# Two casts moved to ScalarE, and the last batch's q and k transposed by DMA instead of TensorE

## The chip, the cores and the metric

The kernel runs on one core of one Trainium2 chip. A core has five engines that run their own instruction streams in order and meet through semaphores: TensorE (PE; its weight loads are listed apart as PEld), VectorE (DVE), ScalarE (ACT), GpSimd (POOL) and SyncE (SP). SP only issues DMAs here. POOL issues DMAs too, between its copies. The metric is the device time of one execution in microseconds (us).

## The reference

Two things are computed one after the other. First, attention with a causal window of 64 keys, for 8 batches, 8 heads, 576 positions and a head size of 64:

```
scores = scale * q @ k.T;  mask = (rel >= 0) & (rel < 64)      # rel = query - key
attn = softmax(where(mask, scores, -1e9));  x = attn @ v        # x as [4608 tokens, 512]
```

Then two dense layers over the 4608 tokens:

```
h = x @ w_in          # 512 -> 2048
g = h - tanh(h)
out = g @ w_out       # 2048 -> 512, float32
```

Inputs and output are float32; the kernel works in bfloat16 with float32 sums.

## The kernel before

**Units.** Heads are taken in pairs: `g = 4*b + pr` is pair `pr` of batch `b`, 32 pairs in all, and g = 28 to 31 are the last batch's. The tokens of a batch are 9 windows of 64. The dense layers work on chunks `c` of 512 tokens (9 chunks); a chunk's first layer is 16 blocks `m` of 4 matmuls (`hp_mm`, L366), then a tanh on ACT (L371) and a subtraction on DVE (`g_sub`, L378) that writes `gT`; its second layer is 16 steps of 4 matmuls (`yp_mm`, L390), and after every fourth a copy on ACT and a store issued by SP (`y_out`, L395 and L397).

**Order.** Nothing is planned by a scheduler: the order on each engine is the order in which the program emits. A loop at the end (L593) walks over half-steps `h` from 0 to 351. Each half-step emits one block of a dense layer (`OPS`: from h = 96 on an even h has a first-layer block, an odd one a second-layer step), then the attention work filed under that h with `at(h, ...)`, and, after a first-layer block, its `g_sub`. So a number given to `at` is a place in every engine's stream, not a time: an engine goes past it as soon as its waits allow. From chunk 2 on, first-layer blocks share two PSUM banks (`m % 2`), in chunk 1 three.

**Attention of one pair.** In the later batches (a is the pair's first half-step, L555 to L567):

- POOL casts q at `a - 7` and k at `a - 5` (`cast`, recorded as L84) from the loaded layout `[head, row, 6*64]` to rows `[96, 6, 128]`, into a tile of a pool of three (`qb`, `kb`).
- `tr` at `a` and `a + 2` (L228 to L239): 6 TensorE transposes (L232) into one PSUM bank. For q, ACT moves head 0's half and DVE head 1's half into `qT` (64x576 each, recorded as L82 and L84); `qT` has a second copy of the width, with zeros in each head's other half. For k, ACT moves 128x576 into `kT`.
- `scores` at a + 5, 7, 9 (3 matmuls L299 and an Exp L301 each), `masking` on DVE at a + 11 (L305), `pv` at a + 13, 14, 15 (3 matmuls L315 each), `norm` on DVE at a + 15 (a reciprocal L322 and two multiplications L326).

`kT` and `qT` each have two buffers, used by `g % 2`. Pairs start 8 half-steps apart: a = 188, 196, 204, 212 for the last batch. Once a batch's four pairs are done, its x is transposed for the first layer, from batch 4 on by two SP DMA transposes (`x_dma`, L347), for batch 6 at h = 196.

The early pairs use `tr_rows` (L247) and `tile_scores` (L262), with the unpadded `qs`: for pair 9, whose k and q were cast on POOL at h = 23 (`cast_pair(9, G)`, L535, ahead of the loads of `w_out` and of batch 3), `tr_rows` stands at 37 and 38 and `tile_scores` at 41 and 43. At h = 39 DVE copies half of batch 2's V windows (`shift_dve(2, 0, 4)`, two copies L154, 64x2080 bf16 from SBUF to SBUF).

**Loads.** POOL issues them. q and k of batch 7 are loaded whole (`load_all`, L98; 576 KB of bf16 each) at h = 168 and 171, its V at h = 158. Before each of these loads a `pace` (L427, recorded as L430) makes POOL wait until DVE has written the newest `gT` block.

**V.** POOL casts V into `vb` pair by pair (`cast_v`; batch 7 at h = 164, 169, 174, 179), nine SP DMAs `keys_v` (L148; batch 7 at h = 182 to 186) copy `vb` into the key windows `vw`, and one DMA `shift_v` (L156; h = 189) fills the other half. `VALUES` (L554) holds these places.

Of the kernel before, what the change touches and what calls it, by code (L numbers as in the profile page):

```python
# [8 lines left out]
BF16 = mybir.dt.bfloat16  # L9
# [6 lines left out]
def kernel(  # L16
# [9 lines left out]
    nc = tc.nc  # L26
    B, H, S, D = q.shape
    NP = H // 2
    NJ = S // 64
    E, P = 6, S // 6  # L30
# [12 lines left out]
    const = ctx.enter_context(tc.tile_pool(name="const", bufs=1))  # L43
# [4 lines left out]
    sm_pool = ctx.enter_context(tc.tile_pool(name="sm", bufs=3))  # L48
    xt_pool = ctx.enter_context(tc.tile_pool(name="xt", bufs=3))
    g_pool = ctx.enter_context(tc.tile_pool(name="g", bufs=2))  # L50
    psum = ctx.enter_context(tc.tile_pool(name="psum", bufs=1, space=PSUM))

    ps = psum.tile([128, 8, 512], F32, name="ps")
# [7 lines left out]
    WIDE = 1024, 1024  # L63
    w_in_sb = [const.tile([128, 4, n], BF16, name=f"wi{i}") for i, n in enumerate(WIDE)]
    w_out_sb = const.tile([128, M, d_model], BF16, name="w_out_sb")
    NR, NPT = 2, 4

    vw = [const.tile([128, NJ, H, D + 1], BF16, name=f"vw{i}") for i in range(2)]  # L70
    vb = const.tile([PV, EV, H, D + 1], BF16, name="vb")
    PT = [const.tile([128, NJ, 128], BF16, name=f"pt{i}") for i in range(NPT)]
    kT = [const.tile([128, 64 + S], BF16, name=f"kt{i}") for i in range(NR)]
    qT = [const.tile([128, 2, S], BF16, name=f"qt{i}") for i in range(NR)]
    qs = [const.tile([128, S], BF16, name=f"qs{i}") for i in range(2)]
    xs = [const.tile([128, NJ + 1, NP, D], BF16, name=f"xs{i}") for i in range(2)]

    stage, rows, whole = {}, {}, {}

    def move(eng, o, i):  # L80
        if eng is nc.scalar:
            nc.scalar.activation(o, i, ACT.Copy)  # L82
        else:
            eng.tensor_copy(o, i)  # L84
# [116 lines left out]
    for i in range(2):  # L201
        nc.vector.memset(kT[i][:, 0:64], 0.0)
    nc.vector.memset(vw[0][0:64, 0], 0.0)

# [13 lines left out]
    def tr_heads(g, which, bank, eng):  # L218

        src = stage.pop((g, which))  # L220
        tp = ps[:, bank, :].bitcast(BF16)[:, 0:E * P].rearrange("c (e p) -> c e p", e=E)
        for e in range(E):
            for h in range(2):
                nc.tensor.transpose(tp[64 * h:64 * h + 64, e, :], src[:, h, D * e:D * e + D], ident[:P, :P])
        o = qs[g % 2] if which == "q" else kT[g % NR][:, 64:]
        move(eng, o.rearrange("c (p e) -> c p e", e=E), tp.rearrange("c e p -> c p e"))

    def tr(g, which, bank, *engs):  # L228
        src = rows.pop((g, which)).rearrange("p e h d -> p e (h d)")
        tp = ps[:, bank, :].bitcast(BF16)[:, 0:E * P].rearrange("c (e p) -> c e p", e=E)  # L230
        for e in range(E):
            nc.tensor.transpose(tp[:, e, :], src[:, e, :], ident[:P, :P])  # L232
        t = tp.rearrange("c e p -> c p e")
        if which == "q":
            o = qT[g % NR].rearrange("c h (p e) -> c h p e", e=E)
            move(engs[0], o[0:64, 0], t[0:64])
            move(engs[1], o[64:128, 1], t[64:128])
        else:
            move(engs[0], kT[g % NR][:, 64:].rearrange("c (p e) -> c p e", e=E), t)  # L239

    def pair_of(banks):
        a, b = banks
        return ps[:, a:b + 1:b - a]
# [3 lines left out]
    def tr_rows(g, which, bank, eng):  # L247

        src = rows.pop((g, which)).rearrange("p e h d -> p e (h d)")
        tp = ps[:, bank, :].bitcast(BF16)[:, 0:E * P].rearrange("c (e p) -> c e p", e=E)  # L250
        for e in range(E):
            nc.tensor.transpose(tp[:, e, :], src[:, e, :], ident[:P, :P])
        o = qs[g % 2] if which == "q" else kT[g % NR][:, 64:]
        move(eng, o.rearrange("c (p e) -> c p e", e=E), tp.rearrange("c e p -> c p e"))

    def hides(grp, banks):
        n = GROUPS[grp][1]
        for h in range(2):
            nc.tensor.matmul(ps[:, banks[h], 0:64 * n], ident, hide[:, h].unsqueeze(1).to_broadcast([128, n, 64]),
                             start=True, stop=False)  # L260

    def tile_scores(g, grp, banks, how="hide"):  # L262

        j0, n = GROUPS[grp]
        if how == "hide":
            hides(grp, banks)
        for i in range(n):
            j = j0 + i
            for h in range(2):
                r = slice(64 * h, 64 * h + 64)  # L270
                nc.tensor.matmul(ps[:, banks[h], 64 * i:64 * i + 64], kT[g % NR][r, 64 * j:64 * j + 128],  # L271
                                 qs[g % 2][r, 64 * j:64 * j + 64], start=how == "mask", stop=how == "mask" or i == n - 1)
        o = PT[g % NPT][:, j0:j0 + n].rearrange("p j (h t) -> p h j t", h=2)
        nc.scalar.activation(o, pair_of(banks)[:, :, 0:64 * n].rearrange("p h (j t) -> p h j t", t=64),  # L274
                             ACT.Exp, scale=scale)
# [19 lines left out]
    def scores(g, grp, bank):  # L295
        sp = ps[:, bank, 0:384].rearrange("p (i q) -> p i q", i=3)
        for i in range(3):
            j = 3 * grp + i
            nc.tensor.matmul(sp[:, i, :], kT[g % NR][:, 64 * j:64 * j + 128],  # L299
                             qT[g % NR][:, :, 64 * j:64 * j + 64], start=True, stop=True)  # L300
        nc.scalar.activation(PT[g % NPT][:, 3 * grp:3 * grp + 3, :], sp, ACT.Exp, scale=scale)  # L301

# [121 lines left out]
    def at(h, fn, *args):  # L424
        items.setdefault(h, []).append((fn, args))
# [10 lines left out]
    V, A, G, Y = nc.vector, nc.scalar, nc.gpsimd, nc.sync  # L436
# [111 lines left out]
    at(76, x_tr, 2, 1, 0, 4, 3, V)  # L548
    at(78, x_tr, 2, 1, 4, 9, 3, A)

    LOADS = {4: (75, 77, 79), 5: (106, 109, 102), 6: (140, 144, 126), 7: (168, 171, 158)}
    STEPS = {2: (0, 0, 49, 57), 3: (72, 79, 86, 93), 4: (100, 107, 114, 121), 5: (128, 135, 142, 149)}
    TURNS = {13: (97, 3, 99, 3), 15: (110, 4, 111, 3)}
    VALUES = {3: (66, 1, 71), 4: (88, 1, 93), 5: (110, 2, 120), 6: (132, 5, 150), 7: (164, 5, 182)}  # L554
    for g in range(2 * NP + 2, B * NP):  # L555
        b, pr = divmod(g, NP)
        a = STEPS[b][pr] if b in STEPS else 8 * g - 36
        if b > 2:
            at(a - 7, cast, g, "q")
            at(a - 5, cast, g, "k")  # L560
        at(a, tr, g, "q", 5 if g < 12 else 2 if g < 13 else 3, A, V)
        at(a + 2, tr, g, "k", 3, A)
        for i in range(3):
            at(a + 5 + 2 * i, scores, g, i, 4)
            at(a + 13 + i, pv, g, i)
        at(a + 11, masking, g)
        at(a + 15, norm, g)  # L567
        if g in TURNS:
            h0, b0, h1, b1 = TURNS[g]
            at(h0, x_tr, b, pr // 2, 0, 4, b0, V)  # L570
            at(h1, x_tr, b, pr // 2, 4, 9, b1, A)
        elif b > 3 and pr == NP - 1:
            at(a + 16, x_dma, b)
        if b > 2:
            cv, cs, ky = VALUES[b]
            at(cv + cs * pr, cast_v, b, pr)
        if pr == 0 and b > 2:
            for j in range(NJ):
                if b == 3:
                    at(ky, windows_v, b, j, (G, Y)[j % 2])  # L580
                else:
                    at(ky + j // 2, windows_v if b < 5 else keys_v, b, j, Y)
            if b > 4:
# [4 lines left out]
            for h, f in sorted(((hq, (load_all, b, "q")), (hk, (load_all, b, "k")), (hv, (load_v_all, b))),  # L588
                               key=lambda x: x[0]):
# [51 lines left out]
```

## Time and profile before

| what | value |
|---|---|
| median of 4 runs | 339.02 us (338.83 to 341.17) |
| the profiled execution's own time | 339.02 us |
| its span, first to last instruction | 337.3 us |
| PE busy, DVE busy, ACT busy, POOL busy | 95%, 59%, 56%, 33% of the span |
| mean granted TensorE clock | 0.969 of full speed |

The span is 1.7 us shorter than the time; that rest is start and end. A busy PE is not PE at its peak, but from about 77 us on PE has next to no idle time: the list of PE's waits has 0.4 us after that point. So in this part each instruction taken from PE's stream shortens the span, as long as nothing makes PE wait instead. Before it PE waits now and then for ACT, DVE or DMA. The timeline merges neighbouring instructions of one kind: "0.42 PE L232 ... x6" are six transposes that took 0.42 us from the start of the first to the modelled end of the last; the start of the next row tells better how long PE was held.

### The profile page before, as it was taken

The page shows a single profiled execution, that of the slowest core. Times are in us where ns is not written, and L with a number is a line of the kernel's source. Part 1 is how long each engine was busy: PE and PEld are TensorE (multiplying, and loading weights), DVE is VectorE, ACT ScalarE, POOL GpSimd, SP SyncE. Part 2 cuts the span into 40 slices and gives each one's busy share as a digit, 9 for nine tenths or more (in the row PEclk, how much of TensorE's full clock was granted, in tenths as well). Part 3 has the DMA queues.
Part 4 walks back from the last instruction along what each step waited for, and adds up shares of the span by engine and source line. Part 5 has one row for each costly group of instructions (what it writes and reads, how often), then busy time and mean ns, then how long its engine had stood idle before and what let it go on. Part 6 is the DMA issues. An engine that isn't in the chain of part 4 may idle for free.

```text
span 337.3 us, 6327 instructions
## 1 busy us (share of the span) xinstructions
PE 321.0 (95%) x2482; PEld 179.2 (53%) x2482; DVE 198.3 (59%) x328; ACT 188.5 (56%) x345; POOL 112.5 (33%) x161
## 2 busy tenths in 40 slices
PE   6779799899999999999999999999999999999996
PEld 2553465455555655655555555555555444444444
DVE  4575867994347675767676666666665344444300
ACT  3534688682466666666566666666654444444411
POOL 8842669803940843632723285100000000000000
PEclk9557999999999999999999999999999999999999
DMA  8999995995699189575975892451013100100012
GB/s 156 161 177 207 163 182 95 179 204 108 115 167 187 20 153 217 115 112 131 160 136 114 160 175 77 101 122 59 33 46 71 64 31 31 64 31 31 33 74 81
DMA packets 41365, 38.31 MB, mean 114 GB/s; under 512 B 13544, under 2 KB 34728, under 8 KB 41144
## 3 DMA queue, kind: packets, MB, share of 16 engines
q0 software_dynamic: 21344, 19.73, 38.4%
q1 hardware_dynamic: 19784, 17.89, 20.5%
q8 instruction: 19, 0.31, 0.4%
q10 hardware_dynamic: 208, 0.29, 0.3%
q14 instruction: 10, 0.08, 0.1%
HBM read 36.70 MB, written 9.44 MB: 137 GB/s over the span
## 4 chain that ended last, share of the span: by engine, by line
PE 77%; DVE 9%; DMA 5%; ACT 5%; POOL 2%; issue 1%; DVEq 0%; POOLq 0%
PE ps L390 34%; PE ps L366 31%; DMA wi<-in_moe_w_in_dram 3%; PE ps L315 3%; PE ps L299 3%; PE ps L232 3%; DVE gT L378 2%; DVE xs L326 2%; DMA vall<-in_v_dram 2%; DVE qt L84 2%; ACT qt L82 1%; PE ps L405 1%; POOL vw L148 1%; ACT th L371 1%; DVE vw L154 1%
## 5 line engine op out<-in xcount | busy, mean ns | idle before, releaser
L366 PE MATMUL ps<-xT,wi 128*128 128x512 bf16 x576 | 149.3, 383 | 1.8 <-DVE gT L378 1.1
L390 PE MATMUL ps<-w_out_sb,gT 128*128 128x512 bf16 x560 | 140.8, 379 | 0.0
L378 DVE TENSOR_TENSOR gT<-ps,th 128x512 bf16<-128x512 f32 x144 | 98.4, 689 | 71.6 <-ACT th L371 69.8
L371 ACT ACTIVATE th<-ps 128x512 f32<-128x512 f32 x144 | 86.0, 598 | 82.5 <-PE ps L366 79.8
L366 PEld LDWEIGHTS <-wi 128*128 128x128 bf16 x576 | 60.6, 114 | 48.2 <-issue 6.0
L390 PEld LDWEIGHTS <-gT 128*128 128x128 bf16 x560 | 51.7, 98 | 50.9 <-issue 0.5
L301 ACT ACTIVATE pt<-ps 128x384 bf16<-128x384 f32 x66 | 32.3, 490 | 22.5 <-PE ps L299 22.5
L84 POOL COPY vb<-vall 72x1024 bf16<-72x1024 bf16 x24 | 24.8, 1055 | 39.8 <-DMA vall<-in_v_dram 39.8
L326 DVE TENSOR_TENSOR xs<-ps,rc 64x576 bf16<-64x576 f32 x44 | 33.2, 755 | 1.1
L84 DVE COPY qt<-ps 64x576 bf16<-64x576 bf16 x22 | 16.7, 760 | 25.5 <-ACT qt L82 25.4
L395 ACT ACTIVATE ysb<-ps 128x512 f32<-128x512 f32 x35 | 21.0, 599 | 17.9 <-PE ps L390 17.7
L84 POOL COPY qb<-qall 96x768 bf16<-96x768 bf16 x24 | 20.6, 860 | 24.8 <-DMA qall<-in_q_dram 19.4
L315 PEld LDWEIGHTS <-pt 128*128 128x128 bf16 x198 | 16.5, 98 | 15.3 <-DVE pt L305 0.8
L315 PE MATMUL ps<-vw,pt 128*128 128x130 bf16 x198 | 22.1, 220 | 0.4 <-DVE pt L305 0.4
L299 PE MATMUL ps<-qt,kt 128*128 128x128 bf16 x198 | 21.8, 219 | 0.0
L84 POOL COPY kb<-kall 96x768 bf16<-96x768 bf16 x24 | 20.3, 847 | 1.3 <-PE ps L232 1.3
L299 PEld LDWEIGHTS <-kt 128*128 128x128 bf16 x198 | 15.4, 98 | 8.8 <-issue 0.2
L82 ACT ACTIVATE kt<-ps 128x576 bf16<-128x576 bf16 x26 | 16.9, 652 | 2.1 <-PE ps L232 1.5
L305 DVE TENSOR_TENSOR pt<-pt,ps 128x1152 bf16<-128x1152 bf16 x22 | 16.4, 744 | 0.8 <-ACT pt L301 0.8
L82 ACT ACTIVATE qt<-ps 64x576 bf16<-64x576 bf16 x22 | 14.0, 636 | 1.5 <-PE ps L232 1.5
L274 ACT ACTIVATE pt<-ps 128x640 bf16<-128x640 f32 (+1 forms) x20 | 12.4, 647 | 2.6 <-PE ps L271 2.6
L148 POOL DMA_DIRECT2D vw<-vb x17 | 9.7, 581 | 6.1 <-DVE kb L84 4.5
(75 smaller groups left out, 204.1 us busy)
## 6 DMA issues: line engine op xcount, KB each, us to landing
out_dram<-ysb SPq DMA_DIRECT2D x35, 256.0 KB
vall<-in_v_dram POOLq DMA_DIRECT2D x7, 576.0 KB, 12.5
qall<-in_q_dram POOLq DMA_DIRECT2D x5, 576.0 KB, 10.7
kall<-in_k_dram POOLq DMA_DIRECT2D x5, 576.0 KB, 11.6
vw<-vb SPq DMA_DIRECT2D x39, 65.0 KB
wi<-in_moe_w_in_dram POOLq DMA_DIRECT2D x2, 1024.0 KB, 14.7
w_out_sb<-in_moe_w_out_dram POOLq DMA_DIRECT2D x2, 1024.0 KB, 10.1
kall<-in_k_dram POOLq DMA_DIRECT2D x11, 144.0 KB, 7.9
```

The costliest lines, as they stand in the source:

```text
L82: nc.scalar.activation(o, i, ACT.Copy)
L84: eng.tensor_copy(o, i)
L299: nc.tensor.matmul(sp[:, i, :], kT[g % NR][:, 64 * j:64 * j + 128], qT[g % NR][:, :, 64 * j:64 * j + 64], start=True, stop=True)
L301: nc.scalar.activation(PT[g % NPT][:, 3 * grp:3 * grp + 3, :], sp, ACT.Exp, scale=scale)
L305: nc.vector.tensor_tensor(p, p, mask.unsqueeze(1).to_broadcast([128, 2 * NJ, 64]), ALU.mult)
L315: nc.tensor.matmul(ps[:, 5 + grp, 130 * i:130 * i + 130], PT[g % NPT][:, j, :], vw[b % 2][:, j, 2 * pr:2 * pr + 2, :], start=True, stop=True)
L326: nc.vector.tensor_tensor(xo[r, :, :, pr, :], ov[r, :, :, h, 0:D], rc[r].to_broadcast([64, 3, 3, 64]), ALU.mult)
L366: nc.tensor.matmul(hp, w_in_tile(ki, m), chunk_tile(c)[:, :, ki % 2, 64 * (ki // 2):64 * (ki // 2) + 64], start=(ki == 0), stop=(ki == 3))
L371: nc.scalar.activation(th, hp, ACT.Tanh)
L378: nc.vector.tensor_tensor(gT[c][:, m, :], hp, th, ALU.subtract)
L390: nc.tensor.matmul(yp, gT[c][:, m, s * 128:(s + 1) * 128], w_out_sb[:, m, :], start=(m == 0), stop=(m == M - 1))
L395: nc.scalar.activation(ysb, ps[:, yp_bank(c, s), :], ACT.Copy)
```

## The change

1. `cast_pair(9, ...)` goes from POOL at h = 23 to ACT at h = 34, behind `tile_scores(8, 0)`.
2. Batch 7's q and k are loaded pair by pair (8 DMAs of 144 KB) at `a - 28` = 160, 168, 176, 184, each pair behind one `pace`.
3. They are no longer transposed on TensorE. POOL casts q at `a - 17` and k at `a - 16`; SP writes the rows to a scratch tensor in DRAM (`bounce`, `a - 14` and `a - 13`), and reads it back with a DMA transpose (`tr_dma`, `a - 8` and `a - 7`), k into `kT`, q into the unpadded `qs`; at `a` DVE copies the two halves of `qs` into `qT` (`spread`).
4. `kT` has three buffers, used by `g % 3`.
5. Batch 7's V: the casts at h = 168, 170, 172, 174, the nine `keys_v` at h = 175 to 183, one to a half-step, `shift_v` at h = 186.

```diff
+    dram = ctx.enter_context(tc.tile_pool(name="dram", bufs=2, space=bass.MemoryType.DRAM))
-    NR, NPT = 2, 4
+    NR, NK, NPT = 2, 3, 4
-    kT = [const.tile([128, 64 + S], BF16, name=f"kt{i}") for i in range(NR)]
+    kT = [const.tile([128, 64 + S], BF16, name=f"kt{i}") for i in range(NK)]
...
+    def bounce(g, n):
+        t = dram.tile([S, 128], BF16, tag=n, name=n + "d")
+        nc.sync.dma_start(out=t.rearrange("(p e) c -> p (e c)", e=E),
+                          in_=rows.pop((g, n)).rearrange("p e h d -> p (e h d)"))
+        rows[g, n + "d"] = t
+    def tr_dma(g, n):
+        nc.sync.dma_start(out=qs[g % 2] if n == "q" else kT[g % NK][:, 64:], in_=rows.pop((g, n + "d")),
+                          transpose=True)
+    def spread(g):
+        for h in range(2):
+            r = slice(64 * h, 64 * h + 64)
+            nc.vector.tensor_copy(qT[g % NR][r, h], qs[g % 2][r])
...
-    at(23, cast_pair, 9, G)
+    at(34, cast_pair, 9, A)
...
-    LOADS = {4: (75, 77, 79), 5: (106, 109, 102), 6: (140, 144, 126), 7: (168, 171, 158)}
+    LOADS = {4: (75, 77, 79), 5: (106, 109, 102), 6: (140, 144, 126), 7: (0, 0, 158)}
-    VALUES = {3: (66, 1, 71), 4: (88, 1, 93), 5: (110, 2, 120), 6: (132, 5, 150), 7: (164, 5, 182)}
+    VALUES = {3: (66, 1, 71), 4: (88, 1, 93), 5: (110, 2, 120), 6: (132, 5, 150), 7: (168, 2, 175)}
...
-        if b > 2:
+        if b == B - 1:
+            at(a - 28, pace, a - 28)
+            at(a - 28, load, g, "q", G)
+            at(a - 28, load, g, "k", G)
+            at(a - 17, cast, g, "q")
+            at(a - 16, cast, g, "k")
+            at(a - 14, bounce, g, "q")
+            at(a - 13, bounce, g, "k")
+            at(a - 8, tr_dma, g, "q")
+            at(a - 7, tr_dma, g, "k")
+            at(a, spread, g)
+        elif b > 2:
             at(a - 7, cast, g, "q")
             at(a - 5, cast, g, "k")
-        at(a, tr, g, "q", 5 if g < 12 else 2 if g < 13 else 3, A, V)
-        at(a + 2, tr, g, "k", 3, A)
+        if b < B - 1:
+            at(a, tr, g, "q", 5 if g < 12 else 2 if g < 13 else 3, A, V)
+            at(a + 2, tr, g, "k", 3, A)
...
-                    at(ky + j // 2, windows_v if b < 5 else keys_v, b, j, Y)
+                    at(ky + j // 2 if b < 7 else ky + j, windows_v if b < 5 else keys_v, b, j, Y)
             if b > 4:
-                at(ky + 7, shift_v, b, 0, NJ - 1)
+                at(ky + 7 if b < 7 else ky + 11, shift_v, b, 0, NJ - 1)
```

More of the change, by code (lines that the diff above doesn't have):

```diff
@@ L200 @@
     nc.vector.memset(vb[:, :, :, D], 1.0)
-    for i in range(2):
+    for i in range(NK):
         nc.vector.memset(kT[i][:, 0:64], 0.0)
@@ L224, in tr_heads @@
                 nc.tensor.transpose(tp[64 * h:64 * h + 64, e, :], src[:, h, D * e:D * e + D], ident[:P, :P])
-        o = qs[g % 2] if which == "q" else kT[g % NR][:, 64:]
+        o = qs[g % 2] if which == "q" else kT[g % NK][:, 64:]
         move(eng, o.rearrange("c (p e) -> c p e", e=E), tp.rearrange("c e p -> c p e"))
@@ L238, in tr @@
         else:
-            move(engs[0], kT[g % NR][:, 64:].rearrange("c (p e) -> c p e", e=E), t)
+            move(engs[0], kT[g % NK][:, 64:].rearrange("c (p e) -> c p e", e=E), t)
     def pair_of(banks):
@@ L252, in tr_rows @@
             nc.tensor.transpose(tp[:, e, :], src[:, e, :], ident[:P, :P])
-        o = qs[g % 2] if which == "q" else kT[g % NR][:, 64:]
+        o = qs[g % 2] if which == "q" else kT[g % NK][:, 64:]
         move(eng, o.rearrange("c (p e) -> c p e", e=E), tp.rearrange("c e p -> c p e"))
@@ L270, in tile_scores @@
                 r = slice(64 * h, 64 * h + 64)
-                nc.tensor.matmul(ps[:, banks[h], 64 * i:64 * i + 64], kT[g % NR][r, 64 * j:64 * j + 128],
+                nc.tensor.matmul(ps[:, banks[h], 64 * i:64 * i + 64], kT[g % NK][r, 64 * j:64 * j + 128],
                                  qs[g % 2][r, 64 * j:64 * j + 64], start=how == "mask", stop=how == "mask" or i == n - 1)
@@ L298, in scores @@
             j = 3 * grp + i
-            nc.tensor.matmul(sp[:, i, :], kT[g % NR][:, 64 * j:64 * j + 128],
+            nc.tensor.matmul(sp[:, i, :], kT[g % NK][:, 64 * j:64 * j + 128],
                              qT[g % NR][:, :, 64 * j:64 * j + 64], start=True, stop=True)
@@ L588 @@
             for h, f in sorted(((hq, (load_all, b, "q")), (hk, (load_all, b, "k")), (hv, (load_v_all, b))),
-                               key=lambda x: x[0]):
+                               key=lambda x: x[0])[2 if b == B - 1 else 0:]:
                 at(h, pace, h)
```

## The prediction

> **What bounds the kernel now.** I read the page's shares and slices first, then PE's waits, then the timeline of the two stretches that the change touches: about 55 to 78 us and 183 to 247 us.
>
> ```profile
> span 337.3 us, 6327 instructions
> PE 321.0 (95%) x2482; PEld 179.2 (53%) x2482; DVE 198.3 (59%) x328; ACT 188.5 (56%) x345; POOL 112.5 (33%) x161
> PE   6779799899999999999999999999999999999996
> PEclk9557999999999999999999999999999999999999
> ```
>
> PE is full from the tenth slice on, at a granted clock of 0.9 or more; the profiled execution took 339.02 us, which is also the median, so the sum is made against 339.02. In the late stretch PE goes from one instruction to the next (timeline of PE: start, length, instruction):
>
> ```profile
> 213.03 1.03 PE L366 MATMUL ps<-xT,wi 128*128 128x512 bf16 x4
> 213.90 0.42 PE L232 MATMUL ps<-ident,qb 96*128 96x96 bf16 x6
> 214.15 1.03 PE L390 MATMUL ps<-w_out_sb,gT 128*128 128x512 bf16 x4
> 215.02 0.33 PE L299 MATMUL ps<-qt,kt 128*128 128x128 bf16 x3
> 215.19 1.03 PE L366 MATMUL ps<-xT,wi 128*128 128x512 bf16 x4
> 216.07 0.42 PE L232 MATMUL ps<-ident,kb 96*128 96x96 bf16 x6
> 216.32 1.03 PE L390 MATMUL ps<-w_out_sb,gT 128*128 128x512 bf16 x4
> ```
>
> These are the half-steps 188 to 191, pair 28's transposes. The early stretch is different: ACT, DVE and PE wait for each other in turn (timelines of ACT, PE, DVE and POOL).
>
> ```profile
> 57.28 0.70 ACT L274 ACTIVATE pt<-ps 128x640 bf16<-128x640 f32 x1
> 58.23 0.60 ACT L371 ACTIVATE th<-ps 128x512 f32<-128x512 f32 x1 [0.26 <-PE ps L366]
> 60.22 0.68 ACT L82 ACTIVATE qs<-ps 128x576 bf16<-128x576 bf16 x1
> 60.95 0.32 PE L271 MATMUL ps<-qs,kt 64*128 64x64 bf16 x10 [0.18 <-ACT qs L82]
> 64.51 2.02 PE L366 MATMUL ps<-xT,wi 128*128 128x512 bf16 x8 [0.37 <-DVE gT L378]
> 66.85 0.51 PE L287 MATMUL ps<-vw,pt 128*64 128x65 bf16 x20 [0.33 <-DVE xs L293]
> 61.17 2.56 DVE L154 COPY vw<-vw 64x2080 bf16<-64x2080 bf16 x2
> 62.32 0.84 POOL L84 COPY kb<-kall 96x768 bf16<-96x768 bf16 x1
> 63.09 1.32 POOL L84 COPY qb<-qall 96x768 bf16<-96x768 bf16 x1
> ```
>
> Between 57.28 and 62 us ACT idles 0.26 us only, and PE's scores of pair 9 (60.95) wait for ACT's `qs`. DVE is packed from 61.17 on, and PE waits for it at 64.51 and 66.85. After 66.85 PE has one more wait of 0.37 us (for DVE, at 76.08) before it is full. So what is lost here is handed on to the end.
>
> **PE's transposes, removed.** A plain step from one block of four matmuls to the next takes 0.864 us (254.42 to 255.28 to 256.14 in the late timeline). With q's transposes it takes 214.15 - 213.03 = 1.12, with k's 216.32 - 215.19 = 1.13, so they hold PE 0.256 and 0.266 us. Four pairs: 4 x 0.522 = 2.09 us less. ACT loses four moves of 636 ns and four of 652 ns, DVE four of 760 ns.
>
> **spread, added.** Eight DVE copies 64x576, bf16, SBUF to SBUF. The trace has no such shape. Below: the group 96x768 of that kind took 358 ns, by width 0.27; above: `qt<-ps`, 760 ns. I take 0.3, as kind and source are the first row's. Then a pair's DVE work becomes 0.6 for 0.76 us, and it no longer waits for ACT's half. At half-step 188 DVE is through `norm` at about 215.0; spread to 215.6, `gT` of 188 to 216.3; PE reuses that bank at half-step 192, in the new time 217.19 - 0.52 = 216.67. Slack 0.36 us, cost 0. At 0.76 each the cost is 1.52 - 0.6 - 0.36 = 0.56 a pair, 2.2 in all. The SBUF - State Buffer page of the Trainium skill ("Who interferes with whom") says that a VectorE copy of such a mode and a GpSimd operation exclude each other for a whole instruction. By it a spread that meets a POOL cast (0.83 us) waits up to 0.83, of which PE would see 0.47, and for one pair met the sum would be 0.5 worse; the L154 pair beside POOL's casts (0.78 and 1.86 us) looks like that.
>
> **Bounces and DMA transposes, added; who waits.** SP gets 8 bounces (0.7 us each, as the nine `vw` moves: seven took 4.95) and 8 transposes. SP's `xT` transposes of 2 to 16 blocks took 1.18 to 1.95 us, so 1.25 each for 4.5 blocks: 15.6 us more of SP between 196 and 230 us, beside the 11 us that it has there now (nine V moves 6.3, the shift 0.5, `x_dma` 2.8, four stores 1.3). Behind them on SP stand the output stores; `ysb` has three buffers, 24 half-steps or 25 us, so a store may be some us late for nothing. What matters is when q lands, since DVE waits for it in front of `gT`. Pair 28: its q load (POOL, 185.0, behind V's which lands at 192.0) is cast by 196.5, the bounce goes at 196.5. SP then takes the store at 201.1, k's bounce, five V moves behind POOL's last V cast (about 200.2), and q's transpose at 205.8. Landing has no row for SP; the nearest from above is POOL's 144 KB load, 7.8 us; from below, the `xT` transposes, whose bytes had moved 2.6 us after SP was done with them. That gives 209.7 to 213.6; DVE is ready for it at 215.0. Pairs 29 and 31 have at least as much. The tight one is pair 30: its transpose stands behind `x_dma` of batch 6, issued at 222.4 to 225.2 in the new time, so it goes out 225.2 to 226.5 and lands at 229 to 233, against DVE ready at 230.9 (plus the 0.36 of slack). Cost 0 by the lower end, 1.8 by the upper; I take 0, since an SBUF-bound transpose on the same queue is the nearer row.
>
> **POOL in the late stretch.** Six more loads and two more paces cost 8 x 0.67 - 2 x 0.79 + 2 x 0.18 = 4.1 us; POOL idles 7.20 + 3.05 + 5.42 + 1.34 us there, for DMAs and PE. Pair 27's casts come at about 199 and 201 and are needed at 205.4 and 207.6: 0. V's moves earlier: PE needs them at 227; only their place ahead of q's transpose counts, which is in the sum above. The third `kT` buffer: one more 85 ns memset while DVE waits 2.6 us for a load; no wait of the list names `kT`'s reuse: 0.
>
> **Two casts on ACT, added.** ACT's row for 96x768 from SBUF is 842 ns (`kb<-kf`, from f32); by ACT's own slope (490, 598, 703 ns for 384, 512, 640) 768 would be 0.81. Neighbours on ACT overlap by 0.11 (the Exp at 58.73 takes 0.59, the next starts at 59.21), so two take 0.84 + 0.73 = 1.57. They sit behind the Exp at 57.28: k is cast 57.87 to 58.71, q 58.60 to 59.44, the tanh of 58.23 starts at 59.33: 1.10 late. Everything behind it on ACT is packed, so `qs` is at 61.32 and PE's scores at 62.05, 1.10 late; on DVE the masked tile, two `gT` and then L154 come 1.10 late too, at 62.27. PE's next meeting with DVE is 64.51 and 66.85, both behind L154.
>
> **Two casts off POOL.** POOL's later work moves up by 1.55 us, so the casts of pairs 10 and 11 run from 60.8 to about 64.3. L154 at 62.27 meets them again: before, its first copy took 0.78, the second 1.86 beside the two casts at 62.32 and 63.09. If it meets none, L154 ends at 63.8, as before, and PE's 0.37 + 0.13 + 0.33 of waiting takes up most of the 1.10: 0.15 lost at 66.85. If both copies meet a cast, 2.6 + 0.8 us: 1.9 lost. I take the old 2.56: 1.10 lost. The earlier loads of `w_out` and batch 3 give nothing: PE waits for none of them.
>
> **Sum.** 339.02 - 2.09 + 1.10 = 338.0 us; with the L154 bounds 337.1 to 338.8.
>
> **Rivals.**
> *The cast is nearly free* (L154 clear of POOL, 0.15 lost): 339.02 - 2.09 + 0.15 = 337.1. For it: POOL is 1.55 earlier and L154 1.10 later, which pulls them apart. Against: POOL's four casts last past 64 us.
> *The transposes land late* (the slower end): the DRAM source makes a transpose hold SP and its data several us. Place: pair 30, DVE waiting in front of `gT`. From a landing 0.36 us after DVE is ready each us is PE's; it ends slower than before by 0.5% when the pairs lose 2.7 us together. At 5 us a transpose in place of 1.25, pair 30's q is out at 230.2 instead of 226.5 and lands near 233 to 237, k 5 us later, just when the scores need it; some 3 us each for pairs 30 and 31: 338.0 + 6 = 344. For it: no trace of DRAM-sourced transposes. Against: the SBUF-sourced ones move 210 GB/s, 147 KB in 0.7 us. Advanced Engine Details and Errata in the Trainium skill ("X-Bar Transpose (TRN2)") calls transposes as fast as other DMAs; no run here shows it for DRAM, and it would leave the sum at 338.0.
> *spread is as dear as a PSUM copy*: 338.0 + 2.2 = 340.2, inside 0.5%.
>
> **How the numbers follow.** 0.5% (1.7 us, 337.3 to 340.7) is what a measurement here can tell from no change. Forecast 338.0: 0.45. Cast nearly free, 337.1: 0.25, faster. spread dear: 0.08. Late transposes: 0.22, slower. So faster 0.25, same 0.53, slower 0.22. The range takes in the first three and the first part of the last: 336.8 to 341.2, leaving out some 0.19; the forecast's own is 337.3 to 338.8.
>
> **What would show it.** Right: PE's L232 groups at 108 instead of 132 each; steps of 0.86 at pairs 28 to 31 and none of PE's waits there; two ACT copies of some 0.84 from `kall` and `qall` at 58 us; pair 9's PV at about 67.9 instead of 66.85; `qt<-qs` near 0.3. Wrong: PE waiting for `gT` behind a DVE copy that waits for a DMA, in 205 to 245; ACT's casts shorter, or L154 at 1.5 together, with PE's 66.85 row in place; or a wait of SP in front of a store that ACT's `ysb` then waits for.

## The result, and the profile after

The changed kernel takes 337.45 us (median of 44 runs, 334.59 to 340.94) beside 339.02 us of the kernel before (median of 63 runs over the same chips, 337.09 to 343.9). The ratio is 0.9946, with a 95% interval of 0.9931 to 0.996: 1.8 us less, give or take 0.5 us. The forecast was 338.0 us, 1.0 us less than before, with 337.3 to 338.8 as its own range. The interval reaches over the bound of 0.5%, so on which side of it the change lies can't be told. The profiled executions of two of the kernels below (`after_pace` and `dma_tr_v_first`; the latter took 829.78 us) were disturbed ones, and no row is read from them.

The page of the kernel after, its span, PE's busy time and PE's 40 slices:

```profile
span 335.9 us, 6258 instructions
PE 318.0 (95%) x2434; PEld 176.6 (53%) x2434; DVE 198.5 (59%) x333; ACT 185.4 (55%) x339; POOL 113.9 (34%) x167
PE   6769899699999999999999999999999999999996
```

PE has 48 transposes less (2482 - 2434) and 3.0 us less to do; its slices are full from the tenth on, as before.

The late stretch of the kernel after, timeline of PE at the half-steps 188 to 191 (start, length, instruction):

```profile
213.75 1.03 PE L383 MATMUL ps<-xT,wi 128*128 128x512 bf16 x4
214.62 1.03 PE L407 MATMUL ps<-w_out_sb,gT 128*128 128x512 bf16 x4
215.48 0.33 PE L316 MATMUL ps<-qt,kt 128*128 128x128 bf16 x3
215.65 1.03 PE L383 MATMUL ps<-xT,wi 128*128 128x512 bf16 x4
216.51 1.03 PE L407 MATMUL ps<-w_out_sb,gT 128*128 128x512 bf16 x4
```

Nothing stands between two blocks any more but the previous pair's scores: from 213.75 to 214.62 the step is 0.87 us and from 215.65 to 216.51 it is 0.86, where before these two were 1.12 and 1.13. DVE and SP in the same stretch:

```profile
214.11 1.52 DVE L343 TENSOR_TENSOR xs<-ps,rc 64x576 bf16<-64x576 f32 x2
215.65 0.62 DVE L131 COPY qt<-qs 64x576 bf16<-64x576 bf16 x2
216.31 0.69 DVE L395 TENSOR_TENSOR gT<-ps,th 128x512 bf16<-128x512 f32 x1
206.92 1.50 SPq L125 DMA_TRANSPOSE qs<-qd  x1
217.37 2.66 SPq L125 DMA_TRANSPOSE qs<-qd  x1
226.49 1.77 SPq L125 DMA_TRANSPOSE qs<-qd  x1
```

The pair's two `spread` copies take 0.62 us together and start as soon as DVE is through `norm` (214.11 + 1.52 = 215.63): no wait for a DMA stands in the row, for pair 28 or for the three that follow. The three SP rows are q's transposes of pairs 28, 29 and 30: 1.50, 2.66 and 1.77 us of SP each. From the start of the SP row to the start of `spread` it is 8.7, 6.2 and 5.0 us, and 7.0 for pair 31: pair 30 has the least.

The early stretch of the kernel after, timelines of ACT, PE, DVE and POOL (the bracket is idle time ahead of the instruction, and what ended it):

```profile
56.37 0.84 ACT L83 ACTIVATE kb<-kall 96x768 bf16<-96x768 bf16 x1
57.10 0.84 ACT L83 ACTIVATE qb<-qall 96x768 bf16<-96x768 bf16 x1
57.26 0.43 PE L269 MATMUL ps<-ident,kb 96*128 96x96 bf16 x6 [0.34 <-ACT kb L83]
60.51 0.32 PE L288 MATMUL ps<-qs,kt 64*128 64x64 bf16 x10 [0.84 <-ACT qs L83]
62.66 1.02 PE L383 MATMUL ps<-xT,wi 128*128 128x512 bf16 x4 [1.82 <-DVE gT L395]
67.64 0.51 PE L304 MATMUL ps<-vw,pt 128*64 128x65 bf16 x20 [0.30 <-DVE xs L310]
58.93 3.07 DVE L295 TENSOR_TENSOR pt<-pt,mask_sb 128x512 bf16<-128x512 bf16 x1 [1.32 <-ACT pt L291]
63.23 1.31 DVE L171 COPY vw<-vw 64x2080 bf16<-64x2080 bf16 x2
59.32 0.87 POOL L85 COPY kb<-kall 96x768 bf16<-96x768 bf16 x1
60.09 0.86 POOL L85 COPY qb<-qall 96x768 bf16<-96x768 bf16 x1
60.85 0.86 POOL L85 COPY kb<-kall 96x768 bf16<-96x768 bf16 x1
61.62 1.06 POOL L85 COPY qb<-qall 96x768 bf16<-96x768 bf16 x1
```

The casts are where they were forecast, 0.84 us each and overlapping by 0.11. PE waits 0.84 us for `qs` behind them. Before that it waits 0.34 us for `kb` at 57.26. But what then holds PE longest, 1.82 us at 62.66, is not behind the V copies (L171, 1.31 us, clear of POOL). It is behind the masked tile at 58.93: an operation of this shape takes 0.42 us at 66.18 in the same profile, and lasted 3.07 us here, until 62.00. POOL's four casts run from 59.32 to 62.68 without a gap beside it; the first three are over at 61.72, and the fourth takes 1.06 us in place of some 0.86.

To compare stretches, three times are read from each profile: **E**, the start of pair 8's first masked scores on PE; **M**, from there to pair 9's second PV (the x20 row that stands at 66.85 in the profile before); **L**, from that PV to the end of the span.

| kernel | pair 9's casts | E | M | L |
|---|---|---|---|---|
| before | POOL | 56.89 | 9.96 | 270.45 |
| `before_again` | POOL | 55.77 | 10.65 | 270.4 |
| `cast_act_only` | ACT | 54.71 | 11.36 | 270.3 |
| after | ACT | 55.39 | 12.25 | 268.3 |
| `after_v_first` | ACT | 55.61 | 10.58 | 268.2 |
| `late_tr` | ACT | 56.82 | 10.74 | 273.1 |
| `dma_tr_only` | POOL | 55.84 | 10.10 | 269.6 |
| `dma_tr_again` | POOL | 55.51 | 9.98 | 269.5 |
| `dve_casts` | DVE | 57.12 | 8.79 | 269.0 |
| `dve_casts_v_first` | DVE | 56.06 | 8.87 | 269.8 |
| `dma_tr_two_batches` | DVE | 56.82 | 8.80 | 274.1 |
| `before_pace` | POOL | 55.61 | 12.04 | 272.05 |

From before to after E falls by 1.50, M rises by 2.29 and L falls by 2.19: 1.4 us of span. E differs by 1.12 us between two executions of the same program (56.89 and 55.77), it lies between 54.71 and 57.12 in the kernels of this table in no order that the edits explain, and ahead of it hardly anything is changed. So that part is taken for scatter, not for the change's.

### The profile page after: what moved, and what is told of

It is laid out like the page before. It is cut to its first block, busy times and chain, and to the rows that moved or that the text cites. A ratio compares the mean times of both kernels' runs of the same rounds, so it can differ in the third digit from the quotient of the medians.

```text
span 335.9 us, 6258 instructions
## 1 busy us (share of the span) xinstructions
PE 318.0 (95%) x2434; PEld 176.6 (53%) x2434; DVE 198.5 (59%) x333; ACT 185.4 (55%) x339; POOL 113.9 (34%) x167
## 4 chain that ended last, share of the span: by engine, by line
PE 74%; DMA 9%; DVE 7%; ACT 5%; POOL 2%; issue 2%; DVEq 0%; POOLq 0%
PE ps L407 34%; PE ps L383 29%; DMA qall<-in_q_dram 5%; DMA vall<-in_v_dram 4%; PE ps L332 3%; PE ps L316 3%; DVE xs L343 2%; PE ps L249 2%; DVE gT L395 2%; DVE qt L85 2%; ACT qt L83 1%; PE ps L422 1%; POOL vall L143 1%; ACT th L388 1%; PE ps L349 1%
## 5 line engine op out<-in xcount | busy, mean ns | idle before, releaser
L85 DVE COPY qt<-ps 64x576 bf16<-64x576 bf16 x18 | 13.7, 760 | 24.1 <-ACT qt L83 24.1
L85 POOL COPY qb<-qall 96x768 bf16<-96x768 bf16 x23 | 19.3, 840 | 19.8 <-DMA qall<-in_q_dram 19.8
L85 POOL COPY kb<-kall 96x768 bf16<-96x768 bf16 x23 | 19.1, 830 | 2.1 <-DMA kall<-in_k_dram 2.1
L83 ACT ACTIVATE kt<-ps 128x576 bf16<-128x576 bf16 x22 | 14.4, 653 | 2.1 <-PE ps L249 1.6
L96 POOL DMA_DIRECT2D qall<-in_q_dram x15 | 9.7, 648 | 8.6 <-DMA wi<-in_moe_w_in_dram 4.7
L83 ACT ACTIVATE qt<-ps 64x576 bf16<-64x576 bf16 x18 | 11.5, 638 | 1.4 <-PE ps L249 1.4
```

## The experiments

### One part alone

`cast_act_only` is the kernel before with the first part of the change:

```diff
-    at(23, cast_pair, 9, G)
+    at(34, cast_pair, 9, A)
```

> The kernel before with pair 9's casts on ACT at half-step 34 and nothing else. Measured by the stage M from the start of pair 8's first masked scores to the start of pair 9's PV on PE (before 9.96 us, changed kernel 12.25 us), and by L from there to the end of the span (270.45 and 268.26 us). Port theory (DVE operations that read two SBUF tiles or copy SBUF to SBUF wait while POOL runs its casts back to back, and the earlier POOL casts now meet pair 8's masked tile): M 11 to 12.3, L 270.4, time 339.0 + 1.0 to 2.3. ACT theory (only ACT's 1.57 us matter): M 11.1, time 340.1. If the two casts cost nothing on the mean: M 10.1, ratio 1.000.

Measured: 339.59 us (12 runs) beside 339.23; ratio 1.0015 (0.9991 to 1.004), so -0.3 to +1.4 us. M is 11.36. Two DVE operations are slowed this time (DVE's timeline):

```profile
58.30 1.00 DVE L278 TENSOR_TENSOR pt<-pt,mask_sb 128x512 bf16<-128x512 bf16 x1 [1.33 <-ACT pt L274]
60.53 2.44 DVE L154 COPY vw<-vw 64x2080 bf16<-64x2080 bf16 x2
```

The V copies lie beside POOL's casts, which run from 59.54 to 63.65. The masked tile does not: it is over at 59.30, and what POOL does beside it is issue the loads of k and V of batch 3 (57.93 to 59.57). So the expected meeting of masked tile and casts did not take place here, and the tile was lengthened all the same, to 1.00 us.

`dma_tr_only` is the changed kernel with that part undone, so that the transposes and what goes with them stand alone:

```diff
-    at(34, cast_pair, 9, A)
+    at(23, cast_pair, 9, G)
```

> The changed kernel with pair 9's casts back on POOL at half-step 23; all of the rest of the change stays. Both theories: M 9.96 as before, L 268.3, time 339.0 - 2.1 = 336.9, ratio 0.994. Rival (the 1.5 us that the changed kernel's trace gains ahead of 55 us come from the change, the third kT buffer or the extra memset, not from scatter between executions): ratio 0.989 and pair 8's first masked scores at 55.4 instead of 56.9 us.

Measured: 337.01 us (12 runs) beside 339.23; ratio 0.9944 (0.9916 to 0.9972), 1.9 us less. The late parts bring the whole gain, and the casts on ACT take nothing from it that the means could tell: 0.9944 without them, 0.9946 with them. The profile does not look like that: M is 10.10 in place of 12.25, 2.15 us less, yet the span is only 0.4 us shorter: E is 0.45 later, which is taken for scatter, and L is 269.6 in place of 268.3. PE's timeline has a wait that the kernel after does not have:

```profile
102.06 0.27 PE L332 MATMUL ps<-vw,pt 128*128 128x130 bf16 x2 [1.18 <-DMA vw<-vb]
```

This is a PV of batch 3, waiting for the moves of V into its windows. The last experiments come back to it. The V copies of this kernel (timelines of DVE and POOL):

```profile
60.06 2.31 DVE L171 COPY vw<-vw 64x2080 bf16<-64x2080 bf16 x2
61.49 1.26 POOL L135 DMA_DIRECT2D vall<-in_v_dram  x1
```

POOL's casts begin at 62.74, when the copies are done, and still the copies take 2.31 us in place of 1.31. Beside them stand POOL's issues of the loads of q, k and V of batch 3; that of V takes 1.26 us, where it takes 0.88 in the changed kernel. `dma_tr_again` (2.19 us) and `before_pace` (1.91) show the same. So POOL's issuing of loads goes with slow DVE copies as its casts do, and this was priced nowhere.

`before_again` is a second profile of the kernel before, to see how much one execution differs from the next:

> The kernel before once more, for the scatter between executions: pair 8's first masked scores between 54.7 and 57 us (56.9 in the first trace), M 9.5 to 11 by how POOL's casts fall against DVE's masked tiles and V copies, L 270.4.

Measured: 338.52 us, one run. E is 55.77 and M 10.65; the two V copies took this (DVE's timeline):

```profile
60.00 3.30 DVE L154 COPY vw<-vw 64x2080 bf16<-64x2080 bf16 x2
```

3.30 us beside POOL's casts from 61.13 on, 2.56 in the first profile of the same program, 1.31 in the changed kernel where they meet none. So the kernel before paid for this meeting already, with 1.25 us of DVE's time in one execution and 1.99 in the other. It does not always go against DVE (timelines of DVE and POOL, kernel before):

```profile
64.37 0.48 DVE L278 TENSOR_TENSOR pt<-pt,mask_sb 128x640 bf16<-128x640 bf16 x1
64.36 1.17 POOL L84 COPY kb<-kall 96x768 bf16<-96x768 bf16 x1
```

This masked tile begins just as one cast ends; it takes its usual 0.48 us, and POOL's next cast takes 1.17 in place of some 0.84.

### Keeping POOL's casts off DVE by a wait

If POOL's casts of pairs 10 and 11 start after the V copies, DVE should be free of them. `after_pace` puts a `pace` (POOL waits for the newest `gT` block) ahead of the casts of pair 10 in the changed kernel, `before_pace` does it in the kernel before:

```diff
+    at(41, pace, 41)
     at(44, cast_pair, 10, G)
```

> The changed kernel, with one pace more on POOL ahead of the casts of pairs 10 and 11, so that they start only when DVE has done the two copies of V's windows. Port theory: the masked tile of pair 8 takes 0.5 to 0.6 us instead of 3.07, the two copies 1.5, M 10.1 to 10.5 and the time 1.8 to 2.2 us below a changed kernel whose M is 12.25: 335.8 to 337.3, ratio 0.990 to 0.995. ACT theory: M stays at 11.1 or above.

> The kernel before with the same pace on POOL. Port theory: the two copies of V's windows take 1.5 instead of 2.56 us, PE's waits at 64.5 and 66.9 go, M 9.1 to 9.3, time 339.0 - 0.8 = 338.2, ratio 0.9977. ACT theory: M 9.96, ratio 1.000. Slower than 1.001 if the held-back casts of pair 10 come too late for its transposes.

Measured: `after_pace` 338.64 us, ratio 0.9995 (0.9967 to 1.0023); `before_pace` 340.58 us, ratio 1.0057 (1.0029 to 1.0086). Both are slower than the kernels that they were made from. Timelines of DVE and PE in `before_pace`:

```profile
63.75 2.86 DVE L278 TENSOR_TENSOR pt<-pt,mask_sb 128x512 bf16<-128x512 bf16 x1
67.65 0.51 PE L287 MATMUL ps<-vw,pt 128*64 128x65 bf16 x20 [2.75 <-DVE xs L293]
69.82 1.91 PE L366 MATMUL ps<-xT,wi 128*128 128x512 bf16 x4
```

The casts now ran from 63.21 to 66.32, and the next masked tile that came up, pair 9's second, stood still until 66.61. The wait only moved the collision, to a place closer to PE: 2.75 us of PE's time. The third row shows a second loss: four matmuls held PE for 1.70 us (the next row begins at 71.52) instead of 0.86. The granted clock was 0.69 from 67.6 to 71.6.

### How much cover the DMA transposes have

`late_tr` issues the two transposes five half-steps later:

```diff
-            at(a - 8, tr_dma, g, "q")
-            at(a - 7, tr_dma, g, "k")
+            at(a - 3, tr_dma, g, "q")
+            at(a - 2, tr_dma, g, "k")
```

> The changed kernel with the DMA transposes five half-steps later, q's at a - 3 and k's at a - 2. It measures the cover that hides them. In the changed kernel SP issues pair 28's q at 206.92 us and DVE spreads it at 215.65 without a wait. Theory that the cover is 3 us or more and a transpose lands some 2.6 us after SP is done with it: q of pair 28 now goes out behind pair 29's bounces, at 214 to 216, lands near 218, and DVE stands still 2 to 3 us in front of spread; the same, 1 to 2 us, at pairs 29 to 31, so that PE waits for gT and the time is 4 to 8 us above the changed kernel. Rival (the transposes had far more cover than that, or land within 1 us): no wait, time 337.5.

Measured: 342.4 us, one run; L 273.1, 4.9 us more than in the changed kernel. DVE and PE at pair 28:

```profile
218.36 0.97 DVE L131 COPY qt<-qs 64x576 bf16<-64x576 bf16 x2 [2.80 <-DMA qs<-qd]
220.10 1.85 PE L383 MATMUL ps<-xT,wi 128*128 128x512 bf16 x4 [2.65 <-DVE gT L395]
221.75 1.91 PE L407 MATMUL ps<-w_out_sb,gT 128*128 128x512 bf16 x4
```

Here the chain that the rival "the transposes land late" described is seen: DVE waits 2.80 us for the transpose, `gT` is behind it, PE waits 2.65 us. Pair 30 loses another 0.23 us, after a DVE wait of 0.79; pairs 29 and 31 lose nothing. Then the steps of PE are 1.65 us (220.10 to 221.75) and 1.71, at a granted clock of 0.57 between 220 and 224: twice 0.8 us more. Waits of 2.88 and 1.6 us of slow steps make 4.5 of the 4.9 us. A transposed q was there 6.5 us after its SP row began for pair 28 (211.83 to 218.36) and 3.6 us for pair 30 (233.02 to 236.63). For the kernel as changed, with 8.7, 6.2, 5.0 and 7.0 us from issue to use, this leaves 2.2 us to spare for pair 28 and 1.3 for pair 30, an estimate that takes each to need as long there as here. A transpose of pair 30 as slow as that of pair 28 would have been waited for.

### The casts on an engine with idle time

In the profile before, DVE has gaps of about 1 us ahead of 56.33 and 58.01 us, well before POOL's casts of pairs 10 and 11, and a cast of this shape takes DVE about 0.35 us. `dve_casts` puts the casts of pairs 9 and 10 there and lets POOL cast pair 11 only behind a `pace`:

```diff
-    at(34, cast_pair, 9, A)
+    at(31, cast_pair, 9, V)
...
-    at(44, cast_pair, 10, G)
+    at(33, cast_pair, 10, V)
+    at(45, pace, 45)
     at(50, cast_pair, 11, G)
```

> The changed kernel, with pair 9's casts on DVE at half-step 31 and pair 10's on DVE at 33, where DVE waits about 1 us each, and pair 11's on POOL behind a pace that lets DVE do all masked tiles and the V copies first. Port theory: no masked tile over 0.6 us, the two V copies 1.5 together, M 9.0 to 9.4 (before 9.96), 0.7 us below the kernel with the DMA transposes alone: 336.3, ratio 0.9915 to 0.993. Theory that PE's stream bounds this stage and the port only fills slack: M 9.9 or more, ratio 0.994.

Measured: 335.97 us (8 runs) beside 338.23; ratio 0.9929 (0.9898 to 0.9961), faster than the kernel before; against the changed kernel (0.9931 to 0.996) the intervals overlap. M is 8.79, the shortest so far. Timelines of DVE and PE:

```profile
55.40 0.35 DVE L85 COPY kb<-kall 96x768 bf16<-96x768 bf16 x1
59.59 0.42 DVE L295 TENSOR_TENSOR pt<-pt,mask_sb 128x512 bf16<-128x512 bf16 x1 [0.25 <-ACT pt L291]
61.35 1.31 DVE L171 COPY vw<-vw 64x2080 bf16<-64x2080 bf16 x2
65.91 0.51 PE L304 MATMUL ps<-vw,pt 128*64 128x65 bf16 x20
```

With no POOL cast beside them the masked tile takes 0.42 us and the V copies 1.31, and pair 9's PV starts without a wait. The edit also ends POOL's issuing of loads at 61.50, just after the V copies begin, so this run does not tell the two causes apart.

### One more batch by DMA

`dma_tr_two_batches` is `dve_casts` with batch 6 treated like batch 7:

```diff
-    LOADS = {4: (75, 77, 79), 5: (106, 109, 102), 6: (140, 144, 126), 7: (0, 0, 158)}
+    LOADS = {4: (75, 77, 79), 5: (106, 109, 102), 6: (0, 0, 126), 7: (0, 0, 158)}
-        if b == B - 1:
+        if b >= 6:
-        if b < B - 1:
+        if b < 6:
```

> The same as the one with the casts on DVE, and batch 6's q and k too are loaded pair by pair, bounced and transposed by DMA. If TensorE's transposes are worth 0.522 us a pair wherever PE is full: 2.1 us less than with batch 7 alone, 334.2, ratio 0.985 to 0.987. If POOL, SP or the DMA queues are too full between 140 and 185 us (POOL waits for V of batch 6 there): DVE stands still in front of spread, and the gain is 1 us or less, or a loss.

Measured: 340.22 us (7 runs) beside 338.23; ratio 1.0074 (1.0043 to 1.0106). By the price of the first four pairs another 2.09 us of transposes are gone from PE, and it is 4.3 us slower than `dve_casts`. POOL, PE and DVE:

```profile
159.07 1.05 POOL L85 COPY vb<-vall 72x1024 bf16<-72x1024 bf16 x1 [9.14 <-DMA vall<-in_v_dram]
178.16 1.32 DVE L131 COPY qt<-qs 64x576 bf16<-64x576 bf16 x2
193.74 0.27 PE L332 MATMUL ps<-vw,pt 128*128 128x130 bf16 x2 [1.04 <-DMA vw<-vw]
197.16 0.34 PE L316 MATMUL ps<-qt,kt 128*128 128x128 bf16 x3 [3.14 <-DMA kt<-kd]
```

PE waits 3.14 us for k's transpose of pair 25, and 1.04 us for the shift of V. That POOL stands 9.14 us in front of V of batch 6 is not new: in `dve_casts` it stands 9.35 us in front of the same cast. New is that q's and k's casts, bounces and transposes of batch 6 take turns with V's casts on POOL and V's moves on SP: the last of these moves leaves SP at 180.50 in place of 179.47, the shift is issued at 183.43 in place of 181.34, and k's transpose goes out behind the shift, at 184.06. Why PE then waited for it until 197.16, the rows do not tell. And `spread` took 1.32 us where it met POOL's casts of 177.60 and 178.37, and 1.46 at 218.93 beside those of 218.50 and 219.40: more than twice the 0.62 that it takes alone.

### Is there a second bound behind the casts?

`dma_tr_only` had gained 2.15 us in M and lost 1.3 of it in L. The last four runs ask whether that is lasting: `dma_tr_only` once more, and three kernels (it, the changed kernel and `dve_casts`) in which V of batch 3 is loaded ahead of k:

```diff
-    at(23, load_all, 3, "k")
     at(23, load_v_all, 3)
+    at(23, load_all, 3, "k")
```

> The changed kernel with pair 9's casts back on POOL at half-step 23, once more, beside the three kernels that follow. Its first profile had one wait that the changed kernel has not: 1.18 us at 102.06, the PV of batch 3's first pair behind the last moves of V into its windows. Theory (the cast on ACT costs PE some 1.5 us before 67 us, but POOL, rid of the casts, brings V of batch 3 some 1.7 us sooner, 79.80 against 81.51, and so saves most of this wait): the ratio to the kernel before stays at 0.994 to 0.995, the wait for V is there again, 0.5 to 1.5 us, and the span from pair 9's PV to the end is 0.5 to 1.5 us longer than the changed kernel's 268.26. Rival (the wait was one execution's, and the casts are free wherever they stand): no wait at 102 us, and 268.3 us.

> The same kernel with V of batch 3 loaded ahead of k of batch 3. Both are cast on POOL, V's first pair ahead of k. Theory: V's casts start some 3 us sooner and its moves land sooner, the wait at 102 us goes, and the ratio falls by about 1 us in 338, to 0.991. Rival (no lasting wait there): the same ratio as the kernel without the exchange, within 0.1%.

> The changed kernel with V of batch 3 loaded ahead of k. Theory: PE has no wait for V at 102 us in the changed kernel, so there is nothing to remove: ratio 0.9946 as without the exchange, within 0.15%; it is then slower than the kernel with the casts on POOL and the same exchange by some 1 us, which is the cost of the cast on ACT that the wait for V had hidden. Rival (cast free): the two are alike.

> The kernel with the casts of pairs 9 and 10 on DVE, V of batch 3 loaded ahead of k. It had a wait of 0.53 us for V at 101.4. Theory: that goes too, and the ratio is 0.9915 (0.9929 less 0.5 us in 338), the fastest so far; no wait of PE above 0.4 us after pair 9's PV. Rival: 0.9929.

Measured, beside 338.99 us of the kernel before on the same chip:

| kernel | median us (runs) | ratio, 95% interval | as against the same kernel without the exchange |
|---|---|---|---|
| `dma_tr_again` | 337.13 (12) | 0.9955 (0.993 to 0.998) | the same kernel: 0.9944 |
| `dma_tr_v_first` | 336.7 (6) | 0.9914 (0.9885 to 0.9942) | 0.9955: 0.0041 less |
| `after_v_first` | 337.01 (6) | 0.9922 (0.9893 to 0.9951) | 0.9946: 0.0024 less |
| `dve_casts_v_first` | 335.06 (6) | 0.9863 (0.9828 to 0.9898) | 0.9929: 0.0066 less |

`dma_tr_again` has no wait for V at 102 us, against the theory's word, but its L is 269.5 all the same. In PE's timeline the lost time stands 14 us later, at a transpose that waits for a cast on POOL, which POOL had done behind the four V casts of batch 4 (111.14 to 115.18), as soon as that V had landed:

```profile
116.00 0.43 PE L249 MATMUL ps<-ident,qb 96*128 96x96 bf16 x6 [1.04 <-POOL qb L85]
```

`dve_casts_v_first` still has the wait that the exchange should have removed, and a longer one (timelines of POOL and PE):

```profile
80.14 1.05 POOL L85 COPY vb<-vall 72x1024 bf16<-72x1024 bf16 x1 [3.90 <-DMA vall<-in_v_dram]
82.52 0.82 POOL L85 COPY kb<-kall 96x768 bf16<-96x768 bf16 x1 [1.32 <-DMA kall<-in_k_dram]
101.22 0.28 PE L332 MATMUL ps<-vw,pt 128*128 128x130 bf16 x2 [1.36 <-DMA vw<-vb]
```

V's first cast starts sooner (80.14 in place of 81.86), but k is now late, and V's other three casts are behind k's: they start at 83.28, as without the exchange at 83.62. So the edit did not do what it was meant to, and as a test of the theory it is void. All three kernels have lower ratios with it, also the one that had no wait to lose; the intervals of each pair overlap or touch, and nothing here explains it.

What the twelve profiles read here do show looks like a bound. From pair 9's second PV to the start of V's first cast it is 14.8 us in the kernel before (81.64 - 66.85), 14.4 in `before_again`, 13.4 in `cast_act_only`, 12.2 in the changed kernel, 13.3 in `after_v_first`, 14.3 in `late_tr` and 14.5 in `before_pace`, and none of them waits for POOL's casts or V's moves between 80 and 125 us. In `dma_tr_only`, `dma_tr_again`, `dve_casts`, `dve_casts_v_first` and `dma_tr_two_batches` it is 15.6, 16.0, 16.0, 15.2 and 16.3, and each of the five has one such wait, of 1.18, 1.04, 0.53, 1.36 and 0.89 us. So it seems that PE can come to batch 3 only so early, and spends waiting later what it gains beyond that before 67 us. This is read from single profiles; no run moved the bound by itself.

`dve_casts_v_first`, at 335.06 us, is the fastest kernel of the case: 1.4% (1.0 to 1.7) faster than the kernel before.

## Why the prediction was right, and where it was not

**The time.** Forecast 338.0, measured 337.45: inside the forecast's own range. The likeliest class (within 0.5%) and its neighbour (faster) can't be told apart by an interval of 0.9931 to 0.996. The hit is partly luck. The change was forecast at 1.0 us and measured at 1.6 by the medians and 1.8 by the ratio, and 337.1, the sum of the rival "the cast is nearly free", lies nearer to the measured time than 338.0. (That rival's 0.15 does not come out of its own terms: 1.10 less 0.37, 0.13 and 0.33 leaves 0.27, so its sum and the lower bound are 337.2.)

**PE's transposes, 2.09 us: right.** L falls from 270.4 to 268.3, and to 268.2 in `after_v_first`. (PE's waits after 77 us in the profile before are three, of 0.27, 0.28 and 0.39 us, 0.9 together and not the 0.4 that was read from the list; they stand in the kernel after as well and change nothing in the sum.) `dma_tr_only` and `dma_tr_again`, without the casts on ACT, gain 1.9 and 1.5 us.

**`spread` at 0.3: right.** It is 0.31, nearer to the copy from SBUF than to that from PSUM, and the rival that priced it at 0.76 falls. The term that the prediction set beside it, a `spread` that meets POOL's casts, did not come up in the changed kernel; where it did, in `dma_tr_two_batches`, the pair of copies took 1.32 and 1.46 us, 0.70 and 0.84 more, about the 0.83 that was the worst price.

**SP and the late transposes, cost 0: right, and the rival had the right mechanism at the wrong distance.** SP was taken at 1.25 us a transpose; it was 1.13 to 2.66. Pair 28's went out at 206.9 (forecast 205.8), pair 30's at 226.5 (forecast 225.2 to 226.5), and no DVE copy waited. `late_tr` shows that what the rival described happens some five half-steps later. That rival named pair 30 as the tight one; in the changed kernel it is, with 5.0 us from issue to use, though in `late_tr` pair 28 waited longest.

**Two casts on ACT, 1.10 us: the size is right before 67 us, and so is the way by which it reaches PE.** ACT was 1.57 us busier, as worked out. Between E and pair 9's second PV PE waits 0.18 us for ACT in each of the four profiles with the casts on POOL (the kernel before, `before_again`, `dma_tr_only`, `dma_tr_again`), and 1.18 to 1.21 us, for `kb` and `qs`, in each of the four with the casts on ACT (`cast_act_only`, the changed kernel, `after_v_first`, `late_tr`): 1.0 us more every time. What the step had wrong is DVE's part. It had all of the collision at the V copies, taken as unchanged at 2.56 us with bounds of 1.5 and 3.4. In the changed kernel's profile the V copies took 1.31, which was the condition of the rival "the cast is nearly free", and PE paid even so, since the masked tile, which the step took to be 1.10 us late and no more, met the casts and took 3.07. Which operation is caught changes between executions and kernels: the V copies (2.56, 3.30), the masked tile (3.07), the V copies beside POOL's load issues (2.31). PE's waits for DVE in the same stretch scatter from 0.70 to 1.42 us in the first four profiles and from 0.48 to 2.12 in the other four, and are alike in the mean, 1.02 and 1.06. Over the profiles with the casts on POOL, `before_pace` left out, M is 9.96, 10.65, 10.10 and 9.98, in the mean 10.17; with them on ACT it is 11.36, 12.25, 10.58 and 10.74, in the mean 11.23. That is 1.06 us, near the forecast, nearly all of it the wait for ACT; single executions scatter as much as the difference.

**Two casts off POOL, "the earlier loads of `w_out` and batch 3 give nothing": this step failed.** On the means the cast costs less than its price: 339.02 - 2.09 = 336.93 against 337.45 measured leaves 0.5 us in place of 1.10, and against the ratio, which is 337.19, 0.3 us; `cast_act_only` alone has 0.5 (-0.3 to 1.4). The prediction found that PE waits for none of those loads, and took that for a price of nothing. It had not asked how near they were to being waited for. With the casts on POOL PE waits 1.0 to 1.2 us for V or for POOL between 100 and 116 us in `dma_tr_only` and `dma_tr_again`, where V's first cast starts 25.7 and 26.0 us behind E; with POOL rid of them, it starts 24.4 us behind E in the changed kernel, and nothing waits. So part of what the cast on ACT costs before 67 us would come back as a wait that is not there. But in the two profiles of the kernel before, which has its casts on POOL too, V's first cast starts at 24.8 and 25.1 us and nothing waits either: POOL issues V's load 4.2 and 4.4 us behind E there, and 5.7 and 5.5 in `dma_tr_only` and `dma_tr_again`, though the edits hardly touch what comes before that. The place of the casts alone does not decide. That this exchange sets the means is argued from single profiles; the runs that should have shown it on the means did not change what they were meant to change, so why the cast costs less than 1.0 us in the end stays open.

**The price of a meeting of DVE and POOL.** The prediction took from the SBUF - State Buffer page of the Trainium skill ("Who interferes with whom") that a VectorE copy and a GpSimd operation exclude each other for a whole instruction, and priced a meeting at one cast of 0.83 us. The same section also names VectorE operations with two SBUF inputs as contending with GpSimd's reads; the masked tile is one, and the prediction left that out. The traces agree that both are lengthened beside POOL's casts. The price is not one cast: a masked tile of 0.42 us stood through three casts of a row in the changed kernel (3.07 us) and through all four in `before_pace` (2.86), while one that began during a cast in `dma_tr_only` took 0.93, and those of pair 9 in the kernel before took 0.48 and 0.44, with POOL's casts lengthened to 1.17 and 1.01 in their place.

## What to carry to other kernels

Removing instructions from the stream of a full engine paid what the steps said, to 0.1 us, as long as the new route had its data there before it was used; the same edit on one more batch lost 4.3 us, with PE waiting for the route's data. A wait that stands in no list may be one that is only just not there: before pricing an earlier load at nothing, measure by how much it was early. And before moving a row of GpSimd copies, see what else of GpSimd and DVE then stands side by side: here a wait that merely shifted the row caught the next masked tile, and the fastest kernels had the casts in gaps of DVE.

## What the runs showed of the hardware that was not expected

- A DVE operation that meets a row of POOL copies can be passed over several times. The masked tile (128x512, 0.41 to 0.43 us alone) took 3.07 us in the changed kernel, through three casts, and 2.86 in `before_pace`, through four, with POOL's casts at 0.81 to 1.06 us, nearly their usual 0.82. It need not be so: in the kernel before two masked tiles kept 0.48 and 0.44 us and POOL's casts took 1.17 and 1.01, and in `dma_tr_only` a tile that had begun during a cast took 0.93. What decides it is not shown.
- DVE's SBUF copies are also slow beside POOL instructions that only issue loads: the two V copies took 2.31, 2.19 and 1.91 us in `dma_tr_only`, `dma_tr_again` and `before_pace`, where no cast runs beside them, and 1.31 in the changed kernel and in `dve_casts`.
- Three times, after PE has waited 2.65 to 3.14 us, its granted clock over the next 4 us is low: 0.57 in `late_tr`, 0.69 in `before_pace`, 0.61 in `dma_tr_two_batches`; steps of 0.86 us take up to 1.71. After the 1.82 us at 62.66 in the changed kernel it stays at 1.00. So the wait of 2.65 us in `late_tr` cost some 4.3. TensorE: Matmul & The Clock Gate in the Trainium skill ("Part 1: The HAM clock gate") has the clock halved after an idle window of about 3.4 us; here shorter waits were enough.
- Two executions of one program differ by more than 1 us in the first 56 us (E 56.89 and 55.77), and the V copies beside POOL's casts by 0.7 us (2.56 and 3.30). A single profile could not have told the cost of the casts on ACT from scatter.
